# The second MoE's output projection as seven products of 2x2 blocks

## The chip, the cores and the metric

One Trainium2 chip; the kernel runs on one of its cores. The metric is the device time of one execution in microseconds (us), and the time of a kernel is the median of its runs.

A core has five engines with queues of their own, and each engine works through its queue in the order in which the program gave it: TensorE (PE: matmuls, and the loads of their weights, PEld), VectorE (DVE), ScalarE (ACT), GpSimd (POOL) and SyncE (SP, which here only issues DMAs). They wait for each other through semaphores. SBUF is the on-chip memory, PSUM the matmuls' accumulators (eight banks of 128x512 fp32).

## What is computed

Attention with pooled keys and values, then a routed MoE with eight experts, then a second MoE that is dense. The change is in the last one:

```python
def _moe2_ref(x, w1, w2, w3, w_out):
    h = np.maximum(np.maximum(x @ w1, x @ w2), x @ w3)
    return (h @ w_out).astype(np.float32)
```

with 4608 tokens, 512 features of the model and 768 of h. The inputs are fp32, the second MoE's weights fp64. Every matrix product is made from three matmuls: an operand is split in a rounded part (hi, type fp32r) and the rest (lo), and hi·hi + hi·lo + lo·hi are summed in PSUM.

## The kernel before

The kernel has three stretches. Attention and routing fill the first 250 us or so. The first MoE follows until about 668 us: it goes over items of 256 tokens of one expert (18 of them, then items of 128 tokens), each in eight pieces, with matmuls of 128x256. Beside it, two generators are advanced a few steps at a time by `between` (L1388 and on): `conversions` (cv) turns the second MoE's fp64 weights into fp32, one block of 128x256 after the other, and `combinations` (cb) makes the operands of the second MoE's products from them, stores them in DRAM (`wdram`, nine chunks of 1.8 MB, each for one weight matrix and one pair of feature blocks), splits the output weights into `ohi` and `olo`, which stay in SBUF, and splits the first group's tokens (`columns(0, False)`).

The second MoE, `second` (L1599 and on), goes over six groups of 768 tokens. A group has nine *quads* and a projection.

A quad (`quad`) multiplies one chunk's 2x2 blocks of weights with the group's 2x2 blocks of tokens in seven products instead of eight (`PROD` says which weight part meets which token part). Each product is six matmuls of 128x384. Three of the four result blocks are ready within the quad; the fourth, m21, needs product 4, which is deferred into the next quad, behind that quad's products 1 and 5 (`late_`, `finish_block`). ScalarE copies the accumulators that are summed on (`snap`: s1 after product 1, s5 after product 5, s2 after product 6), VectorE adds them up to blocks and takes the maximum over the three weight matrices (`block`). So the quads 3c, 3c+1 and 3c+2 give chunk c of h, for c = 0, 1, 2, as four blocks: m11 and m12 (the first and second half of the tokens) of feature block c, m21 and m22 of feature block c + 3. When a block is final, `finish_parts` casts it to hi (ScalarE, into `ghi`) and makes lo (VectorE, into `glo`).

The projection multiplies h with the output weights: for each of the six token tiles j of 128 tokens, six feature blocks times three terms, 18 matmuls of 128x512 into one bank of `po_` (`out_part`). The first two tiles start with the four feature blocks that are ready (`FO`), then comes the deferred product 4, then the rest. ScalarE scales each tile by the tokens' gate, and GpSimd stores its rows by an indirect DMA (`out_rows`). Beside it the next group's tokens are split by VectorE and ScalarE (`columns`, `sums`), advanced by two steps per token tile.

Weight chunks are loaded three ahead (`load_chunk`, three buffers); the load for a freed buffer is issued by SP right after the deferred product 4. The order of all work is the order of the code: nothing reorders it afterwards.

## Time and profile before

| | |
|---|---|
| median of 3 runs | 1223.13 us (1222.7 to 1223.82) |
| the profiled execution | 1221.31 us |
| its span, first to last instruction | 1219.6 us |
| TensorE, matmuls | busy 1188.9 us, 97% |
| weight loads | 1145.1 us, 94% |
| VectorE | 792.4 us, 65% |
| ScalarE | 577.1 us, 47% |
| GpSimd | 306.1 us, 25% |
| DMA | 246.47 MB, mean 202 GB/s |

The matmuls overlap, and the profile models their ends; what a matmul costs in a row of them is therefore read from start to start. "idle before <-releaser" at the end of a row of the timeline says how long the engine stood still before it and what released it. L1650 is the quads' matmul line, L1726 the projection's, L1086 and L1134 the first MoE's.

### The profile page before, as it was taken

What the parts mean: (1) busy time and instruction counts of PE and PEld (TensorE: products, weight loads), DVE (VectorE), ACT (ScalarE), POOL (GpSimd) and SP (SyncE); (2) the same over time, 40 slices, a digit from 0 to 9 for tenths busy, and PEclk for the clock granted to TensorE, in tenths of its full rate; (3) what the DMA queues carried; (4) which work ended last, traced back from release to release, by engine and by line L of the source; (5) the groups of instructions that cost most, each with busy time, mean ns of one, the idle gap of its engine ahead of it and who ended that gap; (6) DMA issues with size and microseconds to landing.
All of it is one profiled execution on the core that took longest, in us unless ns stands there. A gap on an engine that the chain in (4) does not pass through costs nothing. (4 is left out here: it accounts for less than half of the span.)

```text
span 1219.6 us, 22419 instructions
## 1 busy us (share of the span) xinstructions
PE 1188.9 (97%) x8251; PEld 1145.1 (94%) x8251; DVE 792.4 (65%) x1601; ACT 577.1 (47%) x1026; POOL 306.1 (25%) x442
## 2 busy tenths in 40 slices
PE   5899999999999999999999999999999999999998
PEld 5899899999999999999998998998998998998996
DVE  6888977977899899987844445454454454454450
ACT  4667665455666666666645223323223223223221
POOL 7976644201212121230002102003003003004001
PEclk9999999999999999999999999999999999999999
DMA  9999664328875447654359574574674674673631
GB/s 295 243 259 240 175 206 167 122 21 240 272 238 195 150 167 245 222 184 149 111 179 341 189 253 196 205 256 178 218 260 169 227 262 159 237 262 149 248 141 54
DMA packets 104352, 246.47 MB, mean 202 GB/s; under 512 B 17446, under 2 KB 70132, under 8 KB 96172
## 3 DMA queue, kind: packets, MB, share of 16 engines
q1 hardware_dynamic: 84844, 183.37, 43.7%
q0 software_dynamic: 19392, 61.61, 16.6%
q8 instruction: 67, 1.10, 0.4%
q14 instruction: 49, 0.40, 0.1%
HBM read 252.49 MB, written 46.98 MB: 246 GB/s over the span
## 5 line engine op out<-in xcount | busy, mean ns | idle before, releaser
L1650 PE MATMUL p<-yhi,wt 128*128 128x384 f32 x1512 | 387.4, 336 | 0.3 <-DVE m L1671 0.3
L1650 PEld LDWEIGHTS p<-yhi,wt 128*128 128x128 f32 x1512 | 273.3, 188 | 1.4 <-DVE m L1671 0.6
L1650 PE MATMUL p<-ylo,wt 128*128 128x384 f32 x756 | 254.0, 336 | 0.0
L1658 ACT COPY s<-p 128x384 f32<-128x384 f32 x162 | 77.5, 479 | 222.0 <-PE p L1650 221.4
L1134 PE MATMUL py<-hhi,wlo 128*128 128x256 f32 x576 | 163.1, 283 | 1.6 <-DVE wlo L1066 1.6
L1134 PE MATMUL py<-hhi,whi 128*128 128x256 f32 x576 | 164.6, 286 | 0.0
L1086 PE MATMUL ph<-xhi,whi 128*128 128x256 f32 x576 | 163.6, 284 | 0.7 <-DVE hlo L1102 0.7
L1086 PE MATMUL ph<-xhi,wlo 128*128 128x256 f32 x576 | 163.1, 283 | 0.7 <-DVE wlo L1066 0.7
L1086 PE MATMUL ph<-xlo,whi 128*128 128x256 f32 x576 | 163.0, 283 | 0.0
L1134 PE MATMUL py<-hlo,whi 128*128 128x256 f32 x576 | 162.9, 283 | 0.0
L1650 PEld LDWEIGHTS p<-ylo,wt 128*128 128x128 f32 x756 | 142.1, 188 | 0.5
L1679 DVE TENSOR_TENSOR blk<-p,s 128x384 f32<-128x384 f32 x108 | 59.7, 553 | 112.4 <-PE p L1650 112.4
L1635 POOL DMA_INDIRECT gt<-gbuf,ix x26 | 37.9, 1459 | 300.5 <-DMA ix<-idbuf 294.1
L1134 PEld LDWEIGHTS py<-hhi,wlo 128*128 128x128 f32 x576 | 110.4, 192 | 1.8 <-DVE wlo L1066 1.8
L1086 PEld LDWEIGHTS ph<-xhi,whi 128*128 128x128 f32 x576 | 110.5, 192 | 0.9 <-DVE hlo L1102 0.9
L1086 PEld LDWEIGHTS ph<-xhi,wlo 128*128 128x128 f32 x576 | 110.5, 192 | 0.9 <-DVE wlo L1066 0.9
L1086 PEld LDWEIGHTS ph<-xlo,whi 128*128 128x128 f32 x576 | 110.5, 192 | 0.0
L1134 PEld LDWEIGHTS py<-hlo,whi 128*128 128x128 f32 x576 | 110.5, 192 | 0.0
L1134 PEld LDWEIGHTS py<-hhi,whi 128*128 128x128 f32 x576 | 110.5, 192 | 0.0
L1066 DVE TENSOR_TENSOR wlo<-w2raw,whi 128x1024 fp32r<-128x1024 f32 x84 | 102.2, 1221 | 8.3 <-ACT whi L1064 8.3
L1066 DVE TENSOR_TENSOR wlo<-w1raw,whi 128x1024 fp32r<-128x1024 f32 x67 | 81.8, 1221 | 29.1 <-ACT whi L1064 28.1
L1064 ACT CAST whi<-w2raw 128x1024 fp32r<-128x1024 f32 x88 | 91.8, 1043 | 7.2 <-PE py L1134 4.2
(328 smaller groups left out, 2242.9 us busy)
## 6 DMA issues: line engine op xcount, KB each, us to landing
wt<-wdram SPq DMA_DIRECT2D x51, 1792.0 KB
w1raw<-in_moe_w_dram SPq DMA_DIRECT2D x88, 512.0 KB
w2raw<-in_moe_w_dram SPq DMA_DIRECT2D x88, 512.0 KB
wdram<-wst POOLq DMA_DIRECT2D x9, 1792.0 KB
ybuf<-yo SPq DMA_DIRECT2D x40, 256.0 KB
cvraw<-in_moe_w_dram POOLq DMA_DIRECT2D x36, 256.0 KB
xbuf<-x SPq DMA_DIRECT2D x16, 512.0 KB
yr<-ybuf SPq DMA_DIRECT2D x20, 384.0 KB
```

What stands on the lines that cost most here:

```text
L1064: nc.scalar.copy(hi, src)
L1066: eng.tensor_tensor(lo, src, hi.bitcast(F32), op=A.subtract)
L1086: nc.tensor.matmul(ps[:, f, :], a_[:, c, fs], b_[:, c, :], start=(n == 0), stop=(n == 3 * DC - 1))
L1134: nc.tensor.matmul(py[:, c // 2, (c % 2) * 256 : (c % 2 + 1) * 256], a_[:, f, c * P : (c + 1) * P], b_[:, f, :], start=(piece == 0 and f = ...
L1635: nc.gpsimd.indirect_dma_start(out=gt[g][:, j : j + 1], out_offset=None, in_=gbuf[:, :], in_offset=bass.IndirectOffsetOnAxis(ap=cols[j], a ...
L1650: nc.tensor.matmul(ps, a_, b_, start=(start and c + n == 0), stop=(c == 1 and n == 2), skip_group_check=True)
L1658: nc.scalar.copy(t, ps)
L1679: tt(src, add[0], add[1], op=A.add)
```

## The change

The projection becomes seven products of 2x2 blocks, too. h is taken as 2x2 blocks per chunk c (the four blocks above), the output weights as 2x2 blocks of 384 features by 256 columns.

- `combinations` makes the four sums of blocks of the output weights (128x768 each) and, for each of the seven weight parts in the order `OORD`, hi and lo in a staging tile, which GpSimd's queue stores to DRAM: three more chunks (9 to 11) instead of `ohi` and `olo` in SBUF. The conversions get 22 steps per item instead of 20.
- The chunk loads go over twelve chunks per group, the last three of them output weights.
- For each chunk c of h there are seven operand parts instead of four blocks: m11, m21, m22 and four sums (`asum`), each with hi and lo. `enqueue` appends their steps to `parts_`, and `pop` takes a number of steps between the blocks of later quads, or between products of the projection for the last chunk. In code order, part 3 is m12 + m22, part 5 is m11 - m12, part 4 is part 3 less m11, part 6 is m21 less part 4.
- `project` runs, for each of three pairs of token tiles, the seven products of nine matmuls of 128x256 each. Products 1, 6, 7 and 4 accumulate in one bank, 5 and 3 in another, 2 in a third. Four of the seven are scaled into the row tile by ScalarE; three are added to it by VectorE (`scalar_tensor_tensor`, a "gated add" in what follows). The deferred product 4 of the last quad comes behind the first two products.
- PSUM: the two `po_` banks are gone; the quads' tags p1 and p3 have three banks each, p2 two.
- A row store is declared independent of the other stores, and the drain of GpSimd's queue stands behind the first of the last three stores.
- `sums` makes one of its subtractions in two pieces.

The core of the diff:

```diff
+                sm = tl["mraw"].tile([P, 4, KH, DH], F32, tag="mraw", name="osum", bufs=2)
...
+                for i, m in enumerate(OORD):
+                    src = right[PROD[m][1]]
+                    st = tl["stage"].tile([P, KH, 2, DH], F32R, tag="wso", name=f"wso{m}", bufs=2)
+                    nc.scalar.copy(st[:, :, 0, :], src)
                     yield
-                split_o(F2C - 1)
+                    gt_(st[:, :, 1, :], src, st[:, :, 0, :].bitcast(F32), op=A.subtract)
...
-                    for _ in range(1 + (half and p_ % 2)):
+                    for _ in range(1 + (p_ % 2 if half else p_ % 4 == 0)):
                         next(cv, None)
...
+            if key == "m11":
+                hi(0, m_)()
+                parts_.append([lo(0, m_)])
+            elif key == "m22":
+                parts_.extend([
+                    [op_(s1, m12, m_, A.add)],
+                    [hi(3, s1), op_(s3, m11, m12, A.subtract)],
+                    [lo(3, s1), hi(5, s3)],
+                    [op_(s2, s1, m11, A.subtract)],
+                    [lo(5, s3), hi(4, s2)],
+                    [lo(4, s2), hi(2, m_)],
+                ])
+            else:
+                parts_.extend([
+                    [lo(2, m22), hi(1, m_)],
+                    [op_(s4, m_, s2, A.subtract)],
+                    [lo(1, m_), hi(6, s4)],
+                    [lo(6, s4)],
+                ])
...
             s2 = snap(p1, "s2", f"s2_{nm}")
+            pops = ((3, 1, 1, 3), (1, 0, 0, 0), (0, 0, 1, n < CH - 1))[n % 3]
+            pop(pops[0])
             product(p2, w_, 2, True)
             block(g, n, (1, 1), (p2, s1))
+            pop(pops[1])
             product(p3, w_, 3, False)
             block(g, n, (1, 2), (p3, s2))
+            pop(pops[2])
             product(p1, w_, 7, False)
             block(g, n, (2, 2), (p1, s5))
+            pop(pops[3])
...
+        def out_product(g, m, t, ps):
+            i = OORD.index(m)
+            for c in range(KH):
...
+                for n, (a_, b_) in enumerate(((ahi, hi), (ahi, lo), (alo, hi))):
                     nc.tensor.matmul(
...
+                tc.declare_no_dep(store, other, reason="a token's row is in one store alone")
...
+                if m in (1, 5, 6, 4):
+                    nc.scalar.activation(dst, ps, AF.Copy, scale=gate)
+                else:
+                    nc.vector.scalar_tensor_tensor(dst, ps, gate, dst, A.mult, A.add)
+                if m in (3, 4):
+                    store_rows(g, ob[j], j)
+                    if m == 4 and t == 0:
+                        nc.gpsimd.drain()
...
+            steps = [(1, 0), (1, 1), (5, 0), (1, 2), (5, 1), (5, 2), (6, 0), (6, 1), (6, 2)]
+            steps += [(2, 0), (3, 0), (2, 1), (3, 1), (2, 2), (3, 2), (7, 0), (7, 1), (7, 2), (4, 0), (4, 1), (4, 2)]
+            for n, (m, t) in enumerate(steps):
+                take(m, t)
+                if n == 0:
+                    pop(3)
+                elif n == 1:
+                    finish_block()
+                elif n > 2:
+                    pop(3)
...
+                if 5 <= n < 17:
+                    next(ahead, None)
```

What this does to two engines' rows is shown at one place, quad 3 of group 1 (the names end in group, quad and a number; s1, s5 and s2 are the snaps, m21 a block, `ghi` and `glo` the operand parts, `asum` the sums). First ScalarE's queue, from the snaps of quad 3 to the next quad's, before:

```order
L1658 COPY s1_1_3_10386<-p1_1_3_10377 128x384
L1658 COPY s5_1_3_10394<-p3_1_3_10379 128x384
L1688 CAST ghi0_9391<-m22_1_0_10244 128x384
L1658 COPY s2_1_3_10413<-p1_1_3_10377 128x384
L1688 CAST ghi0_9391<-m21_1_0_10273 128x384
L1658 COPY s1_1_4_10450<-p1_1_4_10441 128x384
L1658 COPY s5_1_4_10458<-p3_1_4_10443 128x384
```

and now:

```order
L1688 COPY s1_1_3_10544<-p1_1_3_10535 128x384
L1688 COPY s5_1_3_10552<-p5_1_3_10537 128x384
L1688 COPY s2_1_3_10569<-p1_1_3_10535 128x384
L1727 CAST ghi0_9409<-asum_4_10513 128x384 x3
L1727 CAST ghi0_9409<-m22_1_0_10402 128x384
L1727 CAST ghi0_9409<-m21_1_0_10431 128x384
L1727 CAST ghi0_9409<-asum_4_10513 128x384
L1688 COPY s1_1_4_10618<-p1_1_4_10609 128x384
L1688 COPY s5_1_4_10626<-p5_1_4_10611 128x384
```

Two casts became six, all between the snap s2 of quad 3 and the snap s1 of quad 4; the last one takes a sum.

VectorE's queue at the same place, from the maximum for the deferred m21 on (m11, m12 and m22 are the first blocks of quad 3), before:

```order
L1680 TENSOR_TENSOR m21_1_0_10273<-m21_1_0_10273,p1_1_2_10310 128x384
L1689 TENSOR_TENSOR glo0_9392<-m22_1_0_10244,ghi0_9391 128x384
L1671 TENSOR_TENSOR m11_1_3_10421<-p2_1_3_10378,s1_1_3_10386 128x384
L1689 TENSOR_TENSOR glo0_9392<-m21_1_0_10273,ghi0_9391 128x384
L1671 TENSOR_TENSOR m12_1_3_10431<-p3_1_3_10379,s2_1_3_10413 128x384
L1671 TENSOR_TENSOR m22_1_3_10439<-p1_1_3_10377,s5_1_3_10394 128x384
```

and now:

```order
L1708 TENSOR_TENSOR m21_1_0_10431<-m21_1_0_10431,p1_1_2_10468 128x384
L1729 TENSOR_TENSOR asum_4_10513<-m11_1_0_10386,m12_1_0_10394 128x384
L1728 TENSOR_TENSOR glo0_9410<-asum_4_10513,ghi0_9409 128x384
L1729 TENSOR_TENSOR asum_4_10513<-asum_4_10513,m11_1_0_10386 128x384
L1700 TENSOR_TENSOR m11_1_3_10582<-p2_1_3_10536,s1_1_3_10544 128x384
L1728 TENSOR_TENSOR glo0_9410<-asum_4_10513,ghi0_9409 128x384
L1700 TENSOR_TENSOR m12_1_3_10592<-p5_1_3_10537,s2_1_3_10569 128x384
L1728 TENSOR_TENSOR glo0_9410<-asum_4_10513,ghi0_9409 128x384
L1700 TENSOR_TENSOR m22_1_3_10602<-p1_1_3_10535,s5_1_3_10552 128x384
L1728 TENSOR_TENSOR glo0_9410<-m22_1_0_10402,ghi0_9409 128x384
L1729 TENSOR_TENSOR asum_4_10513<-m21_1_0_10431,asum_4_10513 128x384
L1728 TENSOR_TENSOR glo0_9410<-m21_1_0_10431,ghi0_9409 128x384
```

Two lo parts became five in these rows, with three sums between them; the blocks of quad 3 stand among them at every second place.

## Rows read from the trace of the kernel before

**Rows 1.** The page, part 1: busy time, share and instructions of TensorE, first engines.

```profile
PE 1188.9 (97%) x8251; PEld 1145.1 (94%) x8251; DVE 792.4 (65%) x1601; ACT 577.1 (47%) x1026; POOL 306.1 (25%) x442
```

**Rows 2.** Timeline (start, duration, what), TensorE, projection, a token tile's first matmuls.

```profile
1196.60 0.39 PE L1726 MATMUL po<-mohi,ghi 128*128 128x512 f32 x1
...
1200.80 0.39 PE L1726 MATMUL po<-mohi,ghi 128*128 128x512 f32 x1
```

**Rows 3.** Timeline, TensorE, quads 2 and 3 of group 0, one quad apart.

```profile
689.62 0.51 PE L1650 MATMUL p<-yhi,wt 128*128 128x384 f32 x2
...
696.90 0.51 PE L1650 MATMUL p<-yhi,wt 128*128 128x384 f32 x2
```

**Rows 4.** Timeline, TensorE, first MoE, sixteen matmuls in a row.

```profile
566.10 0.28 PE L1086 MATMUL ph<-xhi,whi 128*128 128x256 f32 x1
...
567.90 0.28 PE L1086 MATMUL ph<-xhi,whi 128*128 128x256 f32 x1
```

**Rows 5.** Timeline, ScalarE, quad 3 of group 0: snaps and a cast.

```profile
692.13 0.48 ACT L1658 COPY s<-p 128x384 f32<-128x384 f32 x1 [0.56 <-PE p L1650]
692.51 0.52 ACT L1688 CAST ghi<-m 128x384 fp32r<-128x384 f32 x1
694.21 0.48 ACT L1658 COPY s<-p 128x384 f32<-128x384 f32 x1 [1.19 <-PE p L1650]
```

**Rows 6.** Timeline, VectorE, quad 3 of group 0.

```profile
693.12 0.55 DVE L1680 TENSOR_TENSOR m<-m,p 128x384 f32<-128x384 f32 x1 [0.92 <-PE p L1650]
693.59 0.55 DVE L1689 TENSOR_TENSOR glo<-m,ghi 128x384 fp32r<-128x384 f32 x1
...
697.28 0.56 DVE L1671 TENSOR_TENSOR m<-p,s 128x384 f32<-128x384 f32 x1 [0.48 <-PE p L1650]
```

**Rows 7.** Timeline, TensorE, a wait in quad 1 of group 0.

```profile
677.21 0.45 PE L1650 MATMUL p<-yhi,wt 128*128 128x384 f32 x1 [0.29 <-DVE m L1671]
677.49 0.34 PE L1650 MATMUL p<-ylo,wt 128*128 128x384 f32 x1
```

**Rows 8.** Timeline, TensorE's first projection matmul of group 0, VectorE around it.

```profile
733.48 0.40 PE L1726 MATMUL po<-mohi,ghi 128*128 128x512 f32 x1
...
733.79 0.55 DVE L1689 TENSOR_TENSOR glo<-m,ghi 128x384 fp32r<-128x384 f32 x1
734.26 0.55 DVE L1679 TENSOR_TENSOR blk<-p,s 128x384 f32<-128x384 f32 x1
734.85 0.56 DVE L1680 TENSOR_TENSOR m<-m,blk 128x384 f32<-128x384 f32 x1
```

**Rows 9.** Timeline, VectorE, the next group's y split beside the projection.

```profile
739.13 0.95 DVE L1334 TENSOR_TENSOR ysum<-yr 128x768 f32<-128x768 f32 x1
```

**Rows 10.** Timeline (TensorE, SP) at group 1's projection; stretch 835:836 (last numbers: DMA share, GB/s).

```profile
824.21 0.40 PE L1726 MATMUL po<-mohi,ghi 128*128 128x512 f32 x1
...
828.25 0.33 SPq L1618 DMA_DIRECT2D wt<-wdram  x1
...
835.00:836.00 1.00, 1.00 (x6) 0.77 (x6) 1.00 (x1) 1.00 (x3) 0.97 (x1) 1.00 0.03 1
```

**Rows 11.** First MoE: stretch 440:464 (PE, PEld, DVE, ACT, POOL busy); timeline, VectorE, TensorE.

```profile
440.00:464.00 24.00, 24.00 (x203) 24.00 (x202) 22.56 (x44) 15.71 (x23) 5.70 (x8) 1.00 0.53 188
...
615.88 0.42 DVE L1102 SCALAR_TENSOR_TENSOR hlo<-ph,hhi 128x256 fp32r<-128x256 f32 x1 [5.66 <-ACT hhi L1101]
616.22 0.68 DVE L1346 TENSOR_TENSOR ylo<-ysum,yhi 128x512 fp32r<-128x512 f32 x1
...
668.35 0.41 PE L1650 MATMUL p<-yhi,wt 128*128 128x384 f32 x1
```

**Rows 12.** Timeline, the end: last matmul, last scaling, last store.

```profile
1213.16 0.40 PE L1726 MATMUL po<-mohi,glo 128*128 128x512 f32 x1
...
1213.64 0.69 ACT L1732 ACTIVATE ob<-po,gt 128x512 f32<-128x512 f32 x1 [3.56 <-PEq L1792]
...
1214.70 0.98 POOL L1733 DMA_INDIRECT out_dram<-ob,ix  x1 [2.71 <-ACTq L1792]
```

More of the change, by code (lines that the diff above doesn't have):

```diff
@@ L1605, in second, with bank @@
         g1p = pool(st, "gT", 1)
-        po_ = pool(st, "pout", 2, space=PSUM)
-        pa = pool(st, "pabc", 2, space=PSUM)
+        pa = pool(st, "pabc", 3, space=PSUM)
         tl["yr"] = yp
-        ghi, glo = (g1p.tile([P, F2C, GW], F32R, name=f"{x_}{groups[0]}") for x_ in ("ghi", "glo"))
+        ghi, glo = (g1p.tile([P, KH, 7, HW], F32R, name=f"{x_}{groups[0]}") for x_ in ("ghi", "glo"))
         wt, gt, ix = {}, {}, {}
-        chunks = [(g, n) for g in groups for n in range(CH)]
+        chunks = [(g, n) for g in groups for n in range(NCH)]
+        def bank(m, name):
+            x_ = {1: 1, 2: 2, 5: 3}[m]
+            return pa.tile([P, 512], F32, tag=f"p{x_}", name=name, bufs=2 if x_ == 2 else 3)
         def load_chunk(k_):
@@ L1665, in block @@
             p_, i = divmod(n, 3)
-            f, js = p_ + 3 * (where[0] - 1), slice((where[1] - 1) * HW, where[1] * HW)
             key = f"m{where[0]}{where[1]}"
@@ L1680, in block, with pop, enqueue @@
             tt(mx[key], mx[key], src, op=A.max)
-            finish_parts()
             if i == 2:
-                parts_.append((f, js, mx[key]))
-        def finish_parts():
-            while parts_:
-                f, js, m_ = parts_.pop(0)
-                nc.scalar.copy(ghi[:, f, js], m_)
-                tt(glo[:, f, js], m_, ghi[:, f, js].bitcast(F32), op=A.subtract)
+                enqueue(p_, key, mx[key])
+        asum, whole_m = {}, {}
+        def pop(n=1):
+            for _ in range(min(n, len(parts_))):
+                for step in parts_.pop(0):
+                    step()
+        def enqueue(c, key, m_):
+            whole_m[key] = m_
+            if key == "m12":
+                return
+            if key == "m11":
+                asum[0] = yp.tile([P, 4, HW], F32, tag="ysum", name=uname("asum"), bufs=1)
+            s1, s2, s3, s4 = (asum[0][:, n, :] for n in range(4))
+            m11, m12, m22 = (whole_m.get(x_) for x_ in ("m11", "m12", "m22"))
+            hi = lambda idx, src: lambda: nc.scalar.copy(ghi[:, c, idx, :], src)
+            lo = lambda idx, src: lambda: tt(glo[:, c, idx, :], src, ghi[:, c, idx, :].bitcast(F32), op=A.subtract)
+            op_ = lambda dst, a_, b_, o: lambda: tt(dst, a_, b_, op=o)
+            if key == "m11":
+                hi(0, m_)()
[16 more added lines that the diff above has]
+                ])
         def finish_block():
@@ L1739, in out_rows, with project, take @@
                 oob_is_err=False,
-            )
+            ).ins
+            for other in stores:
+                tc.declare_no_dep(store, other, reason="a token's row is in one store alone")
+            stores.append(store)
+        def project(g, k0, ahead):
+            acc, ob = {}, {}
+            lo_, hi_ = slice(0, DH), slice(DH, DM)
+            def take(m, t):
+                if m in (1, 2, 5):
+                    acc[m, t] = bank(m, f"o{m}_{g}_{t}")[:, 0:DH]
+                if m in (1, 5):
+                    j = t if m == 1 else T3 + t
+                    ob[j] = yp.tile([P, DM], F32, tag="ob", name=f"ob{g}_{j}", bufs=6)
+                ps = acc[{1: 1, 6: 1, 7: 1, 4: 1, 5: 5, 3: 5, 2: 2}[m], t]
+                out_product(g, m, t, ps)
+                j, cols = {1: (t, lo_), 2: (t, lo_), 6: (t, hi_), 3: (t, hi_), 4: (T3 + t, lo_)}.get(m, (T3 + t, hi_))
+                dst, gate = ob[j][:, cols], gt[g][:, j : j + 1]
+                if m in (1, 5, 6, 4):
[16 more added lines that the diff above has]
+                    pop(3)
+                if t == T3 - 1 and m in (6, 3, 4):
+                    k_ = (6, 3, 4).index(m)
+                    wt.pop((g, CH + k_))
+                    load_chunk(k0 + CH + k_ + 3)
+                if 5 <= n < 17:
+                    next(ahead, None)
         for k_ in range(3):
@@ L1748, in second @@
                 pass
+            k0 = groups.index(g) * NCH
             for n in range(CH):
-                quad(g, n, groups.index(g) * CH + n)
+                quad(g, n, k0 + n)
             nxt = g + 1 in groups
@@ L1755, in second @@
                 tokens(g + 1)
[L1756 to L1773 removed]
+            project(g, k0, ahead)
     with ExitStack() as st:
```

84 lines of the change are left out of this document (43 added, 41 removed).

## The prediction

> **What bounds the kernel now.** I read the page first: TensorE is busy 97% of the span [rows 1]. As its ends are modelled, I then read how far apart matmuls start. In the projection 18 matmuls of 128x512 take 4.20 us, 233 ns each [rows 2]; in the quads 42 of 128x384 take 7.28 us, 173 ns each [rows 3]; in the first MoE matmuls of 128x256, each with new weights, start every 120 ns [rows 4]. None of these stretches has a hole, so the second stage lasts as long as its matmuls: per group of 768 tokens nine quads (65.5 us) and a projection of 108 matmuls (25.2 us). VectorE, ScalarE, GpSimd and the DMAs matter only where TensorE comes to wait for them. So the sum is: matmul time saved, less new waits of TensorE, plus what the tail changes.
>
> **The products.** Removed: 6 groups x 108 = 648 matmuls of 128x512, 648 x 0.2333 = 151.2 us [rows 2]. Added: 6 x 7 products x 3 token tiles x 3 chunks x 3 terms = 1134 of 128x256; the nearest rows are the first MoE's, of the same shape and with a weight load each, 0.120 us [rows 4]: 136.1 us. Difference **-15.1 us**, 2.5 per group. That is a tenth and not the eighth of the multiplications, as two starts at 256 columns (240 ns) cost more than one at 512 (233 ns).
>
> The rows stand at 233 and 120 ns. The Trainium skill (TensorE: Matmul & The Clock Gate, Back-to-back issue gap) speaks against this change: it gives a sustained spacing of about 81 ns at 128 columns and 131 ns at 512, by which half the width saves little; an estimate between its two points is 98 ns at 256, and then 189 x 98 ns = 18.5 us stand against 108 x 131 ns = 14.1 us a group, 26 us slower in all. The trace does not agree at 512 columns.
>
> **The convoy between quads.** This is the new wait that I expect. Call u the time from a quad's first matmul; its products take 1.04 us each, in the order 1, 5, 4 of the quad before, 6, 2, 3, 7. Product 6 accumulates onto product 1, so TensorE may start it, wanted at u = 3.12, only when ScalarE has snapped product 1. In the trace a snap starts 0.26 after its product's end (692.13 for product 5, in the quad that starts at 689.79, the second matmul of its row) [rows 3, 5], so this one is done by 1.8. Now ten pieces of operand parts follow chunks 0 and 1 (quads 2 and 5) and are spread over the next quad, and its last cast, of part 6, stands in ScalarE's queue ahead of the snaps of the quad after (first order fence). Follow it in quad 3: the first cast, of part 3, stands behind the snap of product 6, which starts at u = 4.42 (694.21); a cast starts 0.38 after a snap: 4.80, and ends at 5.32 [rows 5]. VectorE then has nine instructions in a row (second fence): lo of part 3 from 5.35, a sum, m11, lo, m12, lo, m22, lo, and the sum for part 6. Independent ones of 128x384 start 0.47 apart [rows 6], so those that wait for TensorE find it done (m22 could start at 7.49, 697.28), and the ninth starts at 5.35 + 8 x 0.47 = 9.11 and ends at 9.66. ScalarE casts part 6 from 9.70; a cast lasts 0.52 and the next instruction starts 0.10 before its end [rows 5], so the snap runs from 10.12 to 10.60. TensorE wants it at 7.28 + 3.12 = 10.40 and gets it at 10.65; a matmul after a wait is followed 0.28 later instead of 0.17 [rows 7], so 0.35 us are lost. This happens after chunks 0 and 1 of six groups, 12 times: **+4.2 us**. Bounds: with a step of 0.44 it is gone (0); with 0.58, the step of dependent instructions (734.26 to 734.85) [rows 8], it is 1.28 each, 15.4.
>
> **The projection's own waits.** Let t be the time from its first matmul. (a) The lo part of m11 for chunk 2 ends at 734.34, t = 0.86 [rows 8]. The old projection takes that chunk later; now product 1's ninth matmul, at t = 0.96, needs it as weights, which load some 0.2 earlier: 0.15 lost, six times, **+0.9**. (b) Part 3, needed first: m22 and the sum end near 2.5, cast 3.0, lo 3.6; the matmul that needs it comes at 4.2, behind two products and the deferred product 4. Nothing. (c) VectorE gets nine gated adds of 128x256 (step 0.34, [rows 11]) beside the split of the next group's y, with four 128x768 instructions of 0.95 for each half [rows 9]. Added up in program order from the last lo part (about 9.3), the adds of product 7 end at 20.2, 21.4 and 22.6; product 4 accumulates into the same banks and wants them at 20.6, 21.7 and 22.8. Zero, with 0.1 to 0.4 to spare; a few percent more on VectorE would cost up to 1 us in each of the five groups that split a next one: 0 to 5. (d) ScalarE has twelve scalings of 128x256 for six of 512, far under its share.
>
> **The loads.** Three more chunks per group, 33 MB. A chunk goes by every 7.28 us, as before, with refills three ahead. The tight one is the third weight chunk, issued after the deferred product 4 and needed by product 3 at t = 12.7. A chunk is issued at this place before too: at 828.25, t = 4.0 after the start at 824.21, behind the y loads, and the DMAs are silent from 835, t = 10.8 [rows 10]. Margin 1.9 us, so nothing; each us beyond it would cost 6.
>
> **The first MoE.** The out weights' split there grows by four sums of 128x768 and has seven lo parts of 768 for six of 512, some 6.4 us of VectorE over about 27 us, and conversions run 22 for 20 steps an item (0.5 us in 24). VectorE has 22.56 of 24 busy at its fullest, TensorE 24.00 of 24 [rows 11]. It is hidden, and cannot gain since no hole is there; if VectorE overflows, 0 to 3 us. The first group's y split ends at 616.9, 51 us ahead of the first quad [rows 11], and stays in the same item in the order. GpSimd gets nine more issues between the gathers, which are made most of an item ahead.
>
> **Row stores.** That they stop waiting for each other gains nothing: TensorE does not wait for them, and the last one waited for ScalarE [rows 12]. At the end three of them now become ready within 2.2 us. Before, the last store starts 1.54 us after the last matmul [rows 12]. Now the scaling is 0.3 shorter, but store 3 (0.98), the drain and store 4 (0.98), each with at least the 0.37 of issue that lies between scaling and store in these rows, stand ahead: the last one starts 0.2 later, and more as the drain empties the engine first; I take **+0.6** (0 to 1.5).
>
> **Sum**: -15.1 + 4.2 + 0.9 + 0.6 = -9.4 us. The profiled execution took 1221.31 us (span 1219.6 and 1.7 around it); from it the changed kernel would take 1211.9. It lies 1.8 under the median, 1223.13; on the median the sum gives 1213.7, my forecast.
>
> **Rivals.** (1) No convoy: steps a little shorter, and -13.6 gives 1209.5. For it: 0.25 us of lateness decides. (2) The projection becomes VectorE's: (c) at 1 us in five groups, 1218.7. For it the thin margins; against it that all its durations are read from rows. (3) The first MoE overflows: +3, 1216.7; against it the 1.4 us free per item. (4) Slower than before: the convoy at the dependent step, 15.4, with the projection on VectorE: 1223.13 - 15.1 + 15.4 + 0.9 + 0.6 + 5 = 1229.9. It decides from 1.1 us per convoy on if (c) stays at zero; against it, rows 6 show 0.47 also behind a read of PSUM. (5) The matmuls do not come at 120 ns: at 133 ns (25.2 / 189) the gain is gone, and at the 173 ns of the 384-wide ones the kernel is 45 us slower, 1268. Against it, rows 4 are of this shape in this kernel. The page's rule above is a case of (5).
>
> **Chances.** Forecast with its neighbourhood (1211 to 1217) 0.52; (1) 0.17; (2) 0.13; (3) 0.08; (4) 0.07; (5) 0.03. The range of eight in ten takes in rivals 1 to 3 and part of the bounds: 1209.0 to 1220.0. A measurement of this kernel tells 0.2% (2.4 us) from no change: faster, under 1220.7, 0.85; within 0.2%, 0.07; slower, 0.08.
>
> **What would show it.** Right: matmuls every 120 ns in the projection, some 23.9 us from its first one to the next group's first, with the deferred product; TensorE idle before product 6 of quads 4 and 7, released by ScalarE's snap, 0.25 us each; nothing else above 1 us. Wrong: idle time before product 4 released by VectorE's gated add (2), waits for `wt` in the projection, holes between 540 and 600 us (3), or no snap waits at all (1).

## The result, and the profile after

| | before | after |
|---|---|---|
| median of 10 runs | 1222.46 us (1220.03 to 1223.82) | 1228.75 us (1226.41 to 1235.17) |
| span of the profiled execution | 1219.6 us | 1226.3 us |
| start to the item that begins near 272 us | 272.6 | 273.1 |
| that item to the first quad | 395.8 | 405.8 |
| first quad to the last matmul | 544.8 | 538.0 |
| last matmul to the end | 6.4 | 9.4 |

The ratio is 1.0059, 95% interval 1.0043 to 1.0076: some 7 us slower, where 9.4 us faster were forecast. The four stretches add up to the spans. The second MoE gained 6.8 us, but the first MoE lost 10.0, and the end 2.9.

The page after, busy times (it answers [rows 1]) and the one costly group of the quads that has idle time before it:

```profile
PE 1183.0 (96%) x8737; PEld 1161.1 (95%) x8737; DVE 884.2 (72%) x1796; ACT 605.4 (49%) x1117; POOL 309.8 (25%) x451
...
L1680 PEld LDWEIGHTS p<-yhi,wt 128*128 128x128 f32 x1512 | 273.5, 188 | 4.5 <-ACT s L1688 4.4
```

VectorE has 92 us more to do; the 4.4 us behind ScalarE's snaps are the convoy. The timeline after, TensorE: the first quad's first matmul (it answers 668.35 in [rows 11]), 43 matmul spacings in the last projection (they answer [rows 2, 4]), two waits of projections, the last matmul ([rows 12]):

```profile
678.94 0.41 PE L1680 MATMUL p<-yhi,wt 128*128 128x384 f32 x1
...
1026.76 0.36 PE L1792 MATMUL o<-wt,ghi 128*128 128x256 f32 x1 [0.71 <-DMA wt<-wdram]
...
1124.44 0.38 PE L1792 MATMUL o<-wt,ghi 128*128 128x256 f32 x1 [0.64 <-DVE ob L1829]
...
1198.83 0.28 PE L1792 MATMUL o<-wt,ghi 128*128 128x256 f32 x1
...
1203.99 0.28 PE L1792 MATMUL o<-wt,glo 128*128 128x256 f32 x1
...
1216.95 0.29 PE L1792 MATMUL o<-wt,glo 128*128 128x256 f32 x1
```

5.16 us over 43 spacings are 120 ns, as forecast. The 10 us are lost in front of 678.94. The stretches of the two items that grew most (stretch; its length; busy time of PE, PEld, DVE, ACT, POOL; granted clock, DMA share, GB/s; [rows 11] has such a row of before):

```profile
347.00:374.00 27.00, 24.27 (x200) 23.66 (x197) 23.71 (x46) 15.06 (x23) 5.96 (x8) 1.00 0.68 234
374.00:399.50 25.50, 24.54 (x204) 24.13 (x203) 24.48 (x47) 16.71 (x25) 6.43 (x8) 1.00 0.48 165
```

An item took 23.9 us before, with TensorE busy throughout; here these two take 27.4 and 25.4. The granted clock stays at 1.00 from 273 us to the last matmul, so what is lost there are holes and not a lower clock. Waits after, from 250 to 680 us (engine, what, released by; us in total, times, longest), and one of them in VectorE's timeline:

```profile
DVE mraw L1219 <- DMA cvraw<-in_moe_w_dram: 7.8, 5, 3.0
...
PE ph L1090 <- DVE hlo L1106: 4.9, 6, 1.9
```

```profile
352.28 0.42 DVE L1240 SCALAR_TENSOR_TENSOR mraw<-cvy,mraw 128x256 f32<-128x256 f32 x1
355.74 0.29 DVE L1219 TENSOR_SCALAR mraw<-cvraw 128x256 int32<-128x256 int32 x1 [3.04 <-DMA cvraw<-in_moe_w_dram]
```

VectorE stands 3.04 us before a conversion whose row has not landed; behind it in the queue are the lo parts of the first MoE, and for these TensorE waits.

The end, in the chain of waits after (start, duration, what):

```profile
1215.63 1.22 POOLq L1833
1216.85 2.48 issue
...
1220.18 0.47 POOL out_dram L1800
```

and before:

```profile
1206.93 1.20 POOLq L1773
1208.13 2.06 issue
```

The drain (1.2 us) is followed by 2.5 us of issue before the next store can go. The last store after:

```profile
1221.47 0.99 POOL L1800 DMA_INDIRECT out_dram<-ob,ix  x1 [0.30 <-issue]
```

It starts 4.52 us after the last matmul; before, 1.54 us [rows 12].

### The profile page after: what moved, and what is told of

It is laid out like the page before. It is cut to its first block, busy times and chain, and to the rows that moved or that the text cites. A ratio compares the mean times of both kernels' runs of the same rounds, so it can differ in the third digit from the quotient of the medians.

```text
span 1226.3 us, 23792 instructions
## 1 busy us (share of the span) xinstructions
PE 1183.0 (96%) x8737; PEld 1161.1 (95%) x8737; DVE 884.2 (72%) x1796; ACT 605.4 (49%) x1117; POOL 309.8 (25%) x451
## 4 chain that ended last, share of the span: by engine, by line
PE 65%; DVE 15%; issue 10%; DMA 5%; ACT 4%; POOL 1%; POOLq 0%; SPq 0%; ACTq 0%; DVEq 0%
PE p L1680 22%; PE py L1138 12%; PE ph L1090 10%; PE o L1792 7%; DVE wlo L1070 3%; PE pav L524 3%; PE ph L1098 2%; PE psc L470 2%; DMA cvraw<-in_moe_w_dram 2%; DVE glo L1728 2%; PE py L1122 2%; PE paT L501 1%; DVE m L1700 1%; PE px L1051 1%; PE pqT L445 1%
## 5 line engine op out<-in xcount | busy, mean ns | idle before, releaser
L1792 PE MATMUL o<-wt,ghi 128*128 128x256 f32 x756 | 137.6, 283 | 2.2 <-DMA wt<-wdram 0.7
L1792 PEld LDWEIGHTS o<-wt,ghi 128*128 128x128 f32 x756 | 117.2, 189 | 3.9 <-ACT ob L1827 1.6
L1665 POOL DMA_INDIRECT gt<-gbuf,ix x26 | 31.2, 1199 | 325.5 <-DMA ix<-idbuf 187.5
L1070 DVE TENSOR_TENSOR wlo<-w2raw,whi 128x1024 fp32r<-128x1024 f32 x84 | 102.2, 1220 | 10.8 <-ACT whi L1068 10.8
```

Source lines behind the costliest of these rows:

```text
L1070: eng.tensor_tensor(lo, src, hi.bitcast(F32), op=A.subtract)
L1665: nc.gpsimd.indirect_dma_start(out=gt[g][:, j : j + 1], out_offset=None, in_=gbuf[:, :], in_offset=bass.IndirectOffsetOnAxis(ap=cols[j], a ...
L1792: nc.tensor.matmul(ps, a_, b_, start=(m in (1, 2, 5) and c + n == 0), stop=(c == KH - 1 and n == 2), skip_group_check=True,)
```

## Experiments: the first MoE

In what follows, M is the time from the item that begins between 270.8 and 274.8 us to the first quad: 395.8 before, 405.8 after. What lies ahead of it differs by up to 4 us between profiled executions of the same code, so M says more than where the first quad stands. M scatters, too: the changed kernel and the four runs below that edit only what comes behind the first MoE (the convoy, the two in the projection, the end) have 405.8, 407.5, 406.1, 406.1 and 404.7. A difference of under 3 us between two profiles is therefore no effect by itself; the lengths of the items and the ratios have to bear it out. Ratios are against the kernel before on the same chip.

**The pace alone, both ways.** In the changed kernel:

```diff
-                    for _ in range(1 + (p_ % 2 if half else p_ % 4 == 0)):
+                    for _ in range(1 + (half and p_ % 2)):
```

> The changed kernel, with the conversions in the first MoE back at 20 steps an item instead of 22, and nothing else. Theory P: the 10.6 us by which the first quad starts later (668.35 before, 678.94 after) come from the faster pace: VectorE, 23.7 of 27 and 24.5 of 25.5 us busy in the items that grew, gets more in an item than fits, and TensorE waits for hlo and wlo parts. Then the first quad starts at 668 to 669 again and the time is 1218 (1228.75 - 10.5). Rival S: the loss comes from the out weights' four sums, seven lo parts and nine stores; then the first quad still starts past 676 and the time is 1226 to 1229.

and the reverse in the kernel before:

> The kernel before, with the conversions at 22 steps an item instead of 20, and nothing else. Theory P (the pace alone makes VectorE overflow): the items between 270 and 550 us grow as they did in the changed kernel, the first quad starts at 676 to 679, the time is 1231 (1222.5 + 8 to 10). Rival S (sums, lo parts and stores of the out weights): 1222 to 1224, the first quad at 668 to 669.

The kernel before at 22 steps: 1230.19 us, 1.0072 (1.0055 to 1.0089), M 406.2. Its items grow like those of the changed kernel (25.8, 27.0, 25.4, 25.5), with the same waits, and so does VectorE's work in them: in the fullest items it is busy 24.1 to 24.6 us here and in the changed kernel, where it was busy 22.4 to 22.5 before. The waits, and the fullest item's stretch:

```profile
DVE mraw L1215 <- DMA cvraw<-in_moe_w_dram: 9.0, 5, 2.9
...
423.80:449.30 25.50, 24.11 (x202) 23.91 (x201) 24.61 (x48) 16.79 (x26) 5.45 (x8) 1.00 0.45 160
```

So a line of the diff that looks like bookkeeping costs 9 us by itself. (Whether their number does it or their place, ahead of an item's first and fifth piece, was not tried.) But the changed kernel at 20 steps gains nothing that stands out from its own 1.0059 (1.0043 to 1.0076): 1226.93, 1.0047 (1.0030 to 1.0064), M 406.2, the time that rival S named. Up to 583 us each item takes 23.9; then come items of 25.4, 16.8 (for 16.1) and 21.9 (for 13.5), the last of these a single item of 128 tokens. The y split, which ended at 628 in the changed kernel, now ends at 642, and one of its loads lands late:

```profile
636.93 0.43 DVE L1358 TENSOR_TENSOR ysum<-yr 128x256 f32<-128x256 f32 x1 [5.81 <-DMA yr<-ybuf]
...
638.03 0.58 PE L1098 MATMUL ph<-xlo,w1raw 128*128 128x128 f32 x1 [4.51 <-DVE hlo L1106]
```

Behind this hole TensorE's granted clock is 0.50, the lower of its two levels (1.2 GHz), until 643.8 us:

```profile
637.00:643.40 6.40, 5.37 (x25) 5.37 (x26) 4.68 (x11) 4.15 (x8) 0.00 (x0) 0.50 0.50 144
```

The next 32 matmuls of 128x128 take 6.3 us there from start to start; 16 took 1.8 us at 629.35, at a clock of 1.00. So of the 8.4 us by which this item is too long, some 4.5 are the hole and some 2.7 the clock.

Theory P held for the kernel before and fell as a way to get the time back: the out weights' added steps lengthen what follows the conversions, and at either pace some part of the whole no longer fits.

**What 22 steps cost: loads that land late, and work.**

```diff
-                        raws[n] = tl["cv"].tile([P, W, 2], I32, tag="cvraw", name=f"cvraw{n}", bufs=2)
+                        raws[n] = tl["cv"].tile([P, W, 2], I32, tag="cvraw", name=f"cvraw{n}", bufs=3)
...
+                load(2)
...
-                    load(n + 2)
+                    load(n + 3)
```

> The changed kernel (conversions at 22 steps an item), with a third buffer for the rows that the conversions load, so that each row is requested one row earlier; nothing else. In the changed kernel VectorE stands for 8.8 us in six waits for these loads between 250 and 560 us, and TensorE's holes lie behind them. Theory B (VectorE's queue stands behind a load that lands late): these waits go, the items between 270 and 550 us take 23.9 to 24.3 us, the first quad starts at 669 to 671, the time is 1219 to 1221. Rival O (22 steps are simply more work than VectorE has room for): the waits for the loads go, but the items stay at 25 us and over, the first quad starts past 676, the time is 1226 to 1229.

1223.96 us, 1.0019 (1.0007 to 1.0031), M 399.8: between the two. From the issue of a row's load until VectorE comes to the row 7.9 us pass in the kernel before, 7.2 in the changed kernel and 12.7 here (means of the 45 or 46 rows whose loads are issued after 265 us). VectorE no longer waits for rows, and 6.0 of the 10.0 us come back; four items stay at 24.3 to 25.4. The first two of those:

```profile
345.50:370.60 25.10, 24.35 (x202) 23.95 (x201) 24.13 (x47) 15.04 (x24) 6.41 (x8) 1.00 0.76 261
370.60:396.00 25.40, 24.46 (x202) 24.05 (x202) 24.38 (x46) 16.64 (x25) 6.44 (x8) 1.00 0.48 165
```

VectorE is busy 24.13 of 25.10 us: it has become the bound. Two tries to relieve it followed. The first moved sums to GpSimd:

```diff
-                        gt_ = nc.vector.tensor_tensor
+                        gt_, gs_ = nc.vector.tensor_tensor, nc.gpsimd.tensor_tensor
-                        gt_(s1, a21, a22, op=A.add)
+                        gs_(s1, a21, a22, op=A.add)
```

and so for s2, s3 and s4.

> The kernel of the run with the third row buffer (22 steps an item, no waits for loads left, first quad at 673.3 instead of 678.9), with the four 128x256 sums of each of the nine weight combinations on GpSimd instead of VectorE, some 1.4 us less for VectorE in each combination. Theory O (the 5 us that stayed are VectorE having more work in an item than fits): the items of 25.2, 25.4, 24.3 and 24.6 us shrink to at most 24.2, the first quad starts at 669 to 671, the time is 1220 to 1221.5. Rival (they come from the order in which parts stand behind casts of ScalarE, or from the GpSimd queue): first quad past 672.5, time 1223 to 1226.

1228.50, 1.0062 (1.0043 to 1.0081), M 407.5: both expectations missed, and the time worse by 4.5 us. Of 93 such VectorE subtractions of 1.22 us in the first MoE (270 to 560 us) seven take 1.45 to 3.51 us, and of 95 in the run with the third row buffer none takes over 1.3; and behind one of the holes the granted clock is 0.50 for 3.3 us (361.2 to 364.5). VectorE and GpSimd in its timeline:

```profile
355.27 0.75 POOL L1266 TENSOR_TENSOR wsum<-mraw 128x256 f32<-128x256 f32 x1
355.46 3.04 DVE L1070 TENSOR_TENSOR wlo<-w1raw,whi 128x1024 fp32r<-128x1024 f32 x1 [1.03 <-ACT whi L1068]
355.97 0.75 POOL L1267 TENSOR_TENSOR wsum<-mraw 128x256 f32<-128x256 f32 x1
356.67 0.74 POOL L1270 TENSOR_TENSOR wsum<-wsum,mraw 128x256 f32<-128x256 f32 x1
357.49 1.59 POOL L1271 TENSOR_TENSOR wsum<-mraw,wsum 128x256 f32<-128x256 f32 x1
358.43 0.94 DVE L1241 SCALAR_TENSOR_TENSOR mraw<-cvy,mraw 128x256 f32<-128x256 f32 x1
```

A VectorE subtraction of 1.22 us takes 3.04 while three GpSimd sums run, and the fourth sum takes 1.59 instead of 0.75 behind it. So this run told nothing on theory O, and the next one left the sums out altogether:

```diff
+                sm = tl["stage"].tile([P, 8, P], F32, tag="wsum", name="wsum")
+                nc.gpsimd.memset(sm, 0.0)
...
-                        gt_(s1, a21, a22, op=A.add)
-                        gt_(s3, a11, a21, op=A.subtract)
...
-                        gt_(s2, s1, a11, op=A.subtract)
-                        gt_(s4, a12, s2, op=A.subtract)
```

> The kernel of the run with the third row buffer (22 steps an item, first quad at 673.3), without the four 128x256 sums of each of the nine weight combinations: the parts are taken from a tile of zeros that is filled once, so this part of the computation is left out. It gives VectorE back some 1.4 us in each combination without giving GpSimd anything to do beside it (with the sums on GpSimd a VectorE split lasted 3.04 us beside them and 1.22 elsewhere, so that run told nothing on this). Theory O (what stayed at 673.3 is VectorE having more work in an item than fits): items between 340 and 550 at most 24.2 us, the first quad at 668.5 to 670.5, the time 1219 to 1221. Rival (the order of casts and parts holds TensorE up, whatever VectorE has to do): items of 25 us stay, first quad past 672, time 1223 to 1225.

1222.31, 1.0004 (0.9994 to 1.0013), M 396.4. The same items:

```profile
346.50:370.70 24.20, 24.18 (x203) 23.98 (x202) 21.68 (x41) 15.00 (x24) 6.25 (x8) 1.00 0.74 253
370.70:394.70 24.00, 24.00 (x202) 23.91 (x201) 22.98 (x42) 16.49 (x25) 6.42 (x8) 1.00 0.50 173
```

With 1.4 to 2.5 us less for VectorE per item TensorE is busy again, and no item takes over 24.3 us. By M, 6.0 of the 10.0 us are waits for rows and 3.4 VectorE's work, and 0.6 stay; by the ratios the two steps give back some 4.9 and 1.8 us. Theory O holds; how much belongs to each part is known to 2 us or so.

**What 20 steps cost: what follows the conversions.**

```diff
+                    over = [next(cv, 1) for _ in range(1 + (half and p_ % 2))]
                     next(cb, None)
+                    if over[0] and half:
+                        next(cb, None)
```

> The changed kernel with the conversions at 20 steps an item, as in the run at that pace, and when they are done the out weights' parts and the first y split go at 24 steps an item instead of 16. Theory L (at 20 steps the loss had only moved: the last conversions end later, so the y split runs to 642 us, among the single items, where its loads stand behind the weight loads on SP's queue and hold VectorE up for 5.8 us): the y split ends by 625, the first quad starts at 669 to 671, the time is 1218 to 1220. Rival: the denser steps are too much for VectorE between 550 and 620, holes appear there, the first quad starts past 674, the time is over 1223.

1224.56, 1.0021 (1.0009 to 1.0034), M 399.7. The y split is early again, but two items near 570 take 26.4 and 25.5. Waits there, 540 to 612 us:

```profile
ACT wso L1302 <- DMA wdram<-wso: 7.8, 4, 2.4
DVE wso L1304 <- ACT wso L1302: 5.8, 5, 1.9
```

The holes came where the rival had them, but not from VectorE's work: ScalarE stands in line for a buffer of an out weight's part whose store has not landed. Some 3 us of this run's time lie elsewhere, in projections that it does not change (541.2 us from first quad to last matmul; see below). Two runs with all mends (those of the second MoE and the end below, the third row buffer, and a step more between this cast and its lo part) still had two of these buffers:

```diff
                     nc.scalar.copy(st[:, :, 0, :], src)
                     yield
+                    yield
                     gt_(st[:, :, 1, :], src, st[:, :, 0, :].bitcast(F32), op=A.subtract)
...
                     yield
-                    yield
```

> All mends together, first MoE by way of few steps: conversions at 20 steps an item with the third row buffer; behind them 24 steps an item, with a step more between ScalarE's cast of an out weight and VectorE's lo part of it (in the run with 24 late steps VectorE stood 5.8 us behind these casts); the last three pieces of a chunk's operand parts spread over the next quad; the drain behind the second row store; the y loads before quad 4, parts also behind the projection's third product, y split one step earlier. If the pieces add up: first quad at 669 to 670.5, quads 64.5 and projections 23.8 to 24.0 us a group, last store 1.5 us after the last matmul, 1228.75 - 9 - 4.1 - 2.6 - 2.5 = 1210.5 us. If the first MoE does not mend (VectorE overfull behind 560): 1214 to 1216.

> As the run with all mends, but the conversions at 21 steps an item and 20 steps an item behind them. If VectorE has room for one step more while the conversions run and wants the late steps thinner, the first quad starts earlier here than in the other one, 668.5 to 669.5, and the time is 1210; if 21 steps already overfill it, items of over 24.2 us appear between 340 and 530 and the time is 1212 to 1214.

At 24 steps 1219.98, 0.9995 (0.9984 to 1.0007), M 407.1; at 21 and 20 steps 1217.75, 0.9972 (0.9959 to 0.9984), M 405.1, with items of 24.8, 25.8 and 24.6 near 380, 430 and 480, and then 26.2 and 26.8. In the first, one item of 35.2 us holds all of the loss: TensorE's waits in it come to 5.9 us, and in three stretches behind them (from 572.6, 579.6 and 589.6 us, 3.4 to 3.6 us each) the granted clock is 0.50 to 0.54. ScalarE's waits from 540 us on begin with

```profile
ACT wso L1303 <- DMA wdram<-wso: 15.7, 5, 4.9
```

The step more brought VectorE out of line, not ScalarE. Then with four of these buffers (and two row buffers again):

```diff
-                    st = tl["stage"].tile([P, KH, 2, DH], F32R, tag="wso", name=f"wso{m}", bufs=2)
+                    st = tl["stage"].tile([P, KH, 2, DH], F32R, tag="wso", name=f"wso{m}", bufs=4)
```

> All mends, with conversions at 20 steps an item and 24 steps behind them, as in the first run with all mends, with two row buffers again and four instead of two buffers for the out weights' parts. In that run one item of 35.2 us held the whole loss, and ScalarE stood 15.7 us there in five waits until a store of an out weight's part had landed, with the casts of the first MoE's weights queued behind. Theory: with four buffers these waits go, the item falls to 24 to 25 us, the first quad starts at 668.5 to 670.5, the time is 1210. Rival (VectorE is overfull there anyway): first quad at 672 to 675, time 1213 to 1215.

> As the run with four buffers for the out weights' parts, but 20 instead of 24 steps an item behind the conversions. If 24 steps overfill VectorE behind 558 us, this one is the better, first quad at 669 to 670, time 1210 to 1211. If the stores were all, both are alike up to 600, and here the last y loads come later, among the weight loads of the single items: VectorE waits 2 to 3 us for one of them and the time is 1212 to 1213.

1217.28, 0.9964 (0.9953 to 0.9975), M 401.1, and 1216.04, 0.9949 (0.9932 to 0.9966), M 401.2. The waits for stores are gone and the items up to 585 us take 23.9 to 24.0, but both expectations missed the next line: one item of 29.4 (28.2). In the first of them, SP's, VectorE's and TensorE's timelines read:

```profile
577.69 3.32 SPq L1017 DMA_DIRECT2D w2raw<-in_moe_w_dram  x2
587.52 2.00 SPq L1341 DMA_DIRECT2D yr<-ybuf  x4
...
595.08 0.43 DVE L1358 TENSOR_TENSOR ysum<-yr 128x256 f32<-128x256 f32 x1 [5.63 <-DMA yr<-ybuf]
...
597.81 0.39 PE L1090 MATMUL ph<-xhi,whi 128*128 128x256 f32 x1 [2.62 <-ACT whi L1068]
```

Here, too, the clock falls behind the hole, to 0.50 from 598.5 to 601.7 us. A stretch of that, and TensorE's rows in it and behind it:

```profile
598.50:601.50 3.00, 2.43 (x11) 2.44 (x12) 2.96 (x6) 2.17 (x5) 0.00 (x0) 0.50 0.02 5
...
599.45 0.41 PE L1090 MATMUL ph<-xhi,whi 128*128 128x256 f32 x1
...
601.37 0.41 PE L1090 MATMUL ph<-xhi,whi 128*128 128x256 f32 x1
...
602.10 0.28 PE L1090 MATMUL ph<-xlo,whi 128*128 128x256 f32 x1
...
603.17 0.28 PE L1090 MATMUL ph<-xlo,whi 128*128 128x256 f32 x1
```

Nine spacings take 1.92 us at a clock of 0.50 and 1.07 at 1.00, 213 ns against 119. By these rows a stretch of 3.2 us at the lower clock, some 15 matmuls, costs some 1.4 us beside the hole (an estimate); the three in the item of 35.2 us cost some 4.6 of the 11.3 that it is too long.

The first y load is issued eight steps ahead of its use, and eight steps had become shorter:

```diff
-                for _ in range(1 if whole_ else 8):
+                for _ in range(1 if whole_ else 14):
```

> The run with four buffers for the out weights' parts and 24 steps behind the conversions, where VectorE's first y sum now comes 14 instead of 8 steps behind the issue of its load; nothing else. In that run the whole loss was one item of 29.4 us, with VectorE standing 5.6 us before the first y sum for its load, which SP's queue had issued behind two weight loads. Theory: this wait goes, the item takes 24 to 25 us, the first quad starts at 669 to 671.5, the time falls from 1217.3 to 1212 to 1213. Rival (the y split comes later now, and its other loads stand between the weight loads of the single items, as in the run at 20 steps): the loss moves behind 610 us and the time stays within 1.5 us.

> The same with 20 instead of 24 steps behind the conversions and 12 instead of 8 steps between the first y load and the first sum. Theory as there, the item of 28.2 us falls to 25 and the time from 1216.0 to 1213; rival as there, and with more weight here, since at this pace the y split ends some 8 us later: 1216 to 1217.

**1210.38 us, 0.9908 (0.9891 to 0.9924)**, M 398.0: this version beats both kernels. The one with 20 steps gives 1215.02, 0.9941 (0.9925 to 0.9958), M 401.1: its long item is gone, but the single items behind it take 18.7 and 16.6 for 16.1 and 13.5, which was the rival. The best one, its first quad, last matmul and last store:

```profile
668.83 0.41 PE L1681 MATMUL p<-yhi,wt 128*128 128x384 f32 x1
...
1200.35 0.29 PE L1793 MATMUL o<-wt,glo 128*128 128x256 f32 x1
...
1201.84 0.98 POOL L1801 DMA_INDIRECT out_dram<-ob,ix  x1 [0.30 <-issue]
```

Its second MoE lasts 531.5 us (before 544.8). M is still 2.2 over before: an item of 26.0, in which VectorE waits 2.4 us for two y loads. By the stretches from the item near 272 us on it gains 13.3 - 2.2 - 0.9 = 10.2 us on the kernel before. The spans of the two profiled executions differ by 11.9; the other 1.7 us lie ahead of that item, where nothing was changed. In the same way the run with eight steps has a span longer by 8.1 us, of which 3.1 are M and 3.9 lie ahead of it, so the longer lead of the y load gives some 3 us by M and 6.9 by the medians.

## Experiments: the second MoE and the end

**The convoy.**

```diff
-            pops = ((3, 1, 1, 3), (1, 0, 0, 0), (0, 0, 1, n < CH - 1))[n % 3]
+            pops = ((3, 1, 1, 1), (1, 1, 1, 0), (0, 0, 1, n < CH - 1))[n % 3]
```

> The changed kernel, with the operand parts of a chunk spread further: the last three pieces behind product 7 of quads 3 and 6 go one each behind product 6, 2 and 3 of the quad after, so that the last cast of a chunk no longer stands ahead of that quad's snaps on ScalarE. Theory: TensorE's wait before product 6 of quads 4 and 7 (0.34 us, 12 times) goes, nine quads of a group take 64.5 instead of 65.2 us, the time is 1224.7 (1228.75 - 4.1). Rival: the moved pieces delay the snaps or blocks of quads 4 and 7 in another place, and the time stays within 1.5 us of the changed kernel.

1223.17, 1.0020 (1.0010 to 1.0029). The changed kernel has TensorE idle before product 6 of quads 4 and 7 in every group, and nine quads take 65.16 us; here they take 64.50 in five groups and 64.57 in the first one, whose first quad and first projection matmul are

```profile
681.04 0.41 PE L1680 MATMUL p<-yhi,wt 128*128 128x384 f32 x1
...
745.61 0.28 PE L1792 MATMUL o<-wt,ghi 128*128 128x256 f32 x1
```

0.66 us in six groups are 4.0 us, 0.33 for each of twelve waits; the forecast was 4.2. The theory holds.

**The loads and VectorE in the projection.** One run issued the y loads before quad 4:

```diff
+                if n == 4:
+                    ahead = columns(g + 1) if nxt else iter(())
+                    next(ahead, None)
                 quad(g, n, k0 + n)
```

> The changed kernel, with the loads of the next group's y issued before quad 4 instead of behind quad 8, and nothing else. In the changed kernel TensorE waits in product 3 of the projections of groups 0, 1 and 3 (0.7, 0.3 and 0.9 us), at the first matmul that reads the third weight chunk. Theory: that chunk lands late because the y loads, 1.6 MB, go ahead of it on the same queue; with them out of the way these waits go, the time falls by 1.5 to 2.5 us to 1226.5, and the waits for VectorE before product 4 (groups 2 and 4) stay. Rival: the chunk is late because the load after it, issued when product 6 is done, shares the DMAs with it; then the waits in product 3 stay within 0.2 us each.

another took the parts and the y split one product earlier:

```diff
-                elif n > 2:
+                elif n > 1:
                     pop(3)
...
-                if 5 <= n < 17:
+                if 4 <= n < 16:
```

> The changed kernel, with three operand parts also taken behind the third product of the projection (5, first token tile), where none were, and the y split one step earlier; nothing else. In the changed kernel VectorE stands 1.5 us in each projection until ScalarE casts a part that is queued behind the scaling of the fourth product, and its queue then runs late up to the adds of product 7, for which product 4 waits (0.6 to 0.8 us in groups 2 and 4). Theory: that hole closes to under 0.5 us, VectorE's adds come 1 us earlier, the waits before product 4 go, and the time falls by 1 to 2 us, to 1227. Rival: the waits before product 4 come from something else in VectorE's queue (the y split, whose loads or casts are late), they stay, and the time stays within 0.5 us.

The first: 1226.60, 1.0033 (1.0021 to 1.0046), and from first quad to last matmul 536.3 instead of 538.0. All that is left of TensorE's waits from 735 us on is

```profile
PE o L1792 <- DVE glo L1728: 0.2, 1, 0.2
```

The waits in product 3 are gone, which the theory said. They stand in all eight other profiles of the changed projection with the y loads behind quad 8 and its parts unmoved, and in none of the six versions above with the loads before quad 4. The waits before product 4, which it expected to stay, are not listed either, though product 4's first matmuls still come 0.1 late. The second: 1226.58, 1.0038 (1.0027 to 1.0048), 537.5 instead of 538.0. VectorE's waits for casts in the projections fall from 15.4 to 9.9 us, as its theory said; product 4 waits no more, and product 3 still does:

```profile
PE o L1792 <- ACT yhi L1360: 0.9, 1, 0.9
PE o L1792 <- DMA wt<-wdram: 0.7, 1, 0.7
```

That product 4 stopped waiting because of either edit is not shown: in the same eight profiles its listed waits for VectorE's gated adds range from none to 2.7 us, and the time from first quad to last matmul in the seven of them that have the changed kernel's quads, too, from 537.0 to 541.2. The 536.3 lie below that range, the 537.5 within it, so by the totals the second edit cannot be told from none. With both (and the spread parts) a projection takes 24.1 us to the next quad in most groups, and 24.2 to 24.5 in a few, where the changed kernel takes 24.2 to 25.1 and the kernel before 26.25.

**The end.**

```diff
-                    if m == 4 and t == 0:
+                    if m == 3 and t == 1:
                         nc.gpsimd.drain()
```

> The changed kernel, with the drain of GpSimd behind the second of the first three row stores of a projection (product 3, second token tile) instead of behind the fourth (product 4, first tile). Theory: at the end the drain and the 2.5 us of issue after it stand ahead of the last two stores, and that is the 2.9 us that the end got longer; without them the last store starts 1.5 to 2 us after the last matmul instead of 4.5, and the time is 1226.1 (1228.75 - 2.6). Rival: the last stores wait for something else (their own writes, the scalings), and the time changes by under 0.7 us.

1226.03, 1.0040 (1.0028 to 1.0053). Last matmul and last store:

```profile
1214.59 0.29 PE L1792 MATMUL o<-wt,glo 128*128 128x256 f32 x1
...
1216.08 0.98 POOL L1800 DMA_INDIRECT out_dram<-ob,ix  x1 [0.31 <-issue]
```

The last store starts 1.49 us after the last matmul instead of 4.52, and from the last matmul to the end it is 7.4 us instead of 9.4. Before it was 6.4; what makes up the last 0.9 us was not tried.

## Why the prediction failed, step by step

- **The first MoE: the step that failed.** The prediction put 0.5 us of added VectorE work against 1.4 us free per item and called the rest hidden. M grew by 10.0 us instead, and 22 steps alone, in the kernel before, cost as much. Two things were wrong in that sum. The work grew by more where it counts: VectorE is busy 24.1 to 24.6 us in the fullest items, 22.4 to 22.5 before, so some 2 us were added where 1.4 were free. And the sum counted busy time only. A queue that is worked through in order also has its waits in it, and the trace of before had them: VectorE waits 6.5 us in five waits for rows there (between 250 and 560 us), without a hole in TensorE. More steps an item use up rows sooner after their request (7.2 us instead of 7.9), and the waits grow to 8.8 us. Rival 3 named an overflow, with 3 us and a chance of 0.08. That is about what the work's part came to (3.4 us by M); the waits' part, 6.0, was left out. It also looked for the holes between 540 and 600 us; they lay between 273 and 546. Rival 4 gave 1229.9, near the measured time, by luck: the convoy of 15.4 us that it rests on measured 4.0.
- **The out weights' steps behind the conversions** were costed at 6.4 us of work, hidden. At 22 steps that held: past 546 us the items take 23.9. What counts is their number: at 20 steps they push the y split past 630 us, where the single items leave no room, and so the quicker pace is what they cost. The prediction took pace and steps for two small terms; they were one.
- **Products**: 120 ns a matmul, right. The gain per group in the best version is 26.25 - 24.09 = 2.2 us (1.8 in one group), for 2.5 forecast; some 0.1 is lost at each of three or four matmuls, most of them at product 4's starts. Why is open.
- **The convoy**: right in place, cause and size, 0.33 for 0.35 each.
- **(a)** The lo part of m11 held TensorE up once (0.2 to 0.3 us) and not six times: too high by 0.6.
- **(c), rival 2**: taken at 0 with a thin margin; product 4 waited in two groups, 0.3 and 0.8 us, and in other profiles of the same projection not at all or up to 2.7 us in all.
- **The loads**: taken at 0 with 1.9 us to spare. The third weight chunk landed some 2.5 us later than the chunk at this place before, and held TensorE up in three groups, 1.9 us in all. That the DMAs fell silent at t = 10.8 before was no margin: three more chunks had to go through, and with the y loads out of their way the waits are gone.
- **The end**: +0.6 forecast, +2.9 found. The price of a drain was taken to be the drain; the 2.06 us of issue behind it, in the chain of waits of before, were not seen. With the drain moved 0.9 of the 2.9 us stay.

Second MoE and end together: forecast -9.4, found -3.9 without mends. With nothing lost in the first MoE the kernel would have come out near 1218.6 (an estimate, 1222.46 - 3.9), faster and inside the stated range. It was the stretch that was argued in a few sentences that decided the sign.

## What to carry to other kernels

Where an engine works in order, count its waits with its work, and when a pace changes, follow each request to its use: the distance in steps stays, the distance in time does not. Background work that is added at the end of a paced list must be followed to where its last step falls. After each mend, look again at which wait ends last: here row loads, VectorE's work, the stores of parts and the y loads stood behind one another, and a version with three of the first MoE's mends still had the M of one with none (407.1 and 405.8). Where a hole of TensorE costs more than its length, look at the granted clock behind it.

## What the runs showed of the hardware that was not expected

- VectorE and GpSimd hold each other up: a 128x1024 subtraction of 1.22 us took 3.04 beside three GpSimd sums of 0.75, and a sum took 1.59 behind it. The Trainium skill (SBUF — State Buffer, SBUF: two separate sides) states that the two engines share a pair of ports as an exclusive lock, for VectorE instructions with two SBUF inputs among others (against a GpSimd instruction that reads SBUF), and that the loser blocks for the whole instruction; the trace agrees: of the 3.04 us, 1.95 pass until the third sum ends at 357.41, and the other 1.09 are about what the subtraction takes alone.
- A drain of GpSimd took 1.2 us, and 2.1 us (before) and 2.5 us (after) of issue followed it in the chain ahead of the next indirect store. Placed behind the second row store, it no longer held up the last one (1.49 us after the last matmul instead of 4.52).
- TensorE's granted clock fell to 0.50 (1.2 GHz) behind holes of the first MoE in some runs, for 3.2 us (a hole of 2.6 us, item of 29.4) and 6.9 us (a hole of 4.5 us, 20 steps); matmuls of 128x256 then started every 213 ns instead of 119. The changed kernel's own profile has no such stretch; those of the convoy run (292.2 to 295.5 us) and of the moved drain (361.2 to 364.5) have one, with the same first MoE.
- A 1.8 MB store on GpSimd's queue stands at 343.38 us, ahead of the row loads that land late near 355 in the changed kernel. That the loads are late because of it was not tried.
